# A hybrid attention and MLP block: the column-tile jobs of w1 in one place, the last k norm ahead of the LN2 statistics, one V drain back on ScalarE

## The chip, the core and the metric

The kernel runs on one core of one Trainium2 chip. The metric is the device time of one launch in microseconds (us). The core's engines work from queues of their own and meet at semaphores: TensorE (PE) multiplies matrices and writes PSUM, VectorE (DVE) and ScalarE (ACT) drain PSUM and do elementwise work, GpSimd (POOL) does elementwise work in SBUF, and SyncE (SP) issues most DMAs.

## The reference

The input x has 2048 tokens of width 448. It is normalised, and two branches are added to it:

```python
xn = layernorm(x)
# A: linear attention, 16 heads of 28
q, k, v = split(xn @ wqkv)
phi_q = concat(softmax(q @ w_phi), softmax(-(q @ w_phi)))   # phi_k alike
kv = phi_k.T @ v ;  z = sum(phi_k) ;  o = (phi_q @ kv) / (phi_q @ z + 1e-6)
A = o @ wo
# B: token mixing and an MLP, on xn
h  = gelu(layernorm(xn) @ w1)                # 448 -> 448
hs = concat(h[:, 0:112] shifted by 1 token, h[:, 112:224] by -1,
            h[:, 224:336] by 2, h[:, 336:448] by -2) @ w2
x1 = xn + hs
B  = x1 + gelu(layernorm(x1) @ w3) @ w4      # 448 -> 1792 -> 448
out = x + A + B
```

## The kernel before

The 2048 tokens are 16 tiles of 128, in groups g of four tiles. Activations are also kept transposed (`xnT`, `hT`, `gT`), so that they can be a matmul's operand. Nearly all matmuls use half of TensorE's rows: a job works on a pair of PSUM banks, with the two row halves running beside each other (64x128 tiles). Each such job comes in two halves, written V(i,0) and V(i,1) below; the second half exchanges rows and banks, and so waits until the matmuls of the first half have ended. There are four pairs of PSUM banks, numbered 0 to 3. A job can start on a pair only when the engine that drains the pair's last job has read it.

The program is a list of operations in the order in which Python calls them; each engine gets its own operations in that order, and a recorder sets the semaphore waits from what each operation reads and writes. So the order of the calls is the order of every queue. Nothing is reordered by a scheduler.

The stages, in order of time:

1. *Front, about 5 to 32 us.* `ln1_stats` and `ln1_apply` normalise x. `xn_T` transposes tiles on TensorE into a bank pair, and ScalarE copies them out (DVE for tiles 10 and 11, in pair 1). Then jobs follow from a list written by hand: V (`v_pair`, x times wv, drained by `v_out` into `vaug`), WA (`wa_pair`, columns 0 to 255 of w1 for one group, drained by `wa_out` with gelu), WC (`wc_pair`, columns 256 to 383, drained by `wc_out`), WD (`wd_pair`, the last 64 columns for half of the tokens, drained by `wd_out`), and FO (`fold_pair`, which folds w_phi into the k and q weights; DVE copies the results to `wpk` and, in four copies a job, to `wpq`). WD is the only job that uses column tiles as well: four 64x64 tiles side by side. Its first half has 16 matmuls, its second 12.
2. *Shifts.* `hop_out`, `hop_in` and `halo` move small strips of `hT` by DMA on SP, in two halves h; the loads of w3, wo and w4 stand behind them in SP's queue.
3. *Eight k/q rounds, about 32 to 69 us.* Round `ps` multiplies k of tiles 2ps and 2ps+1 (pair 1), q (pair 0), and one w2 job (pair 2; V of tiles 12 and 13 in round 0, and V of tiles 14 and 15 in pair 3 beside it). ScalarE takes exp of both signs of k (`k_exp`) and of q (`q_exp`). `k_norm` then sums k's exponentials on DVE (`ksum`), takes the reciprocal on DVE (`rks`) and multiplies on POOL. `w2_out` adds the w2 job to xn on DVE for two tiles (i and i+4), and `ln_stats` takes the LN2 statistics of one tile a round, also on DVE. `ln_scale` turns statistics into scales on POOL (`mv`, `rs`), `g_apply` normalises a tile into `g_tok`, and `g_T` transposes it into `gT` by DMA on SP. `kv_tile` adds phi_k and v of one tile into pair 3.
4. *MLP and output, from about 69 us.* w3 jobs (`a(p)`, `b(p)`) with gelu on ScalarE, the last kv tiles (`K(...)`), `kv_copy` (DVE reads the kv banks), `kv_blocks`, then the numerators (`N`) and the four-part output jobs (`f`).

In the trace each helper has one line: L200 a matmul, L204 a transpose on TensorE, L208 a ScalarE activation, L212 an elementwise operation on DVE or POOL, L215 a DMA transpose, L218 a DMA. So operations are told apart by tile names and shapes. In these names, `w` stands for w1 and what shares its region (the kv copies) as well as for w2, w3 and w4; `g_tok,hi` are the folds; `phik` written by ScalarE from 72 us on is the w3 gelu, which shares phi_k's memory.

At the end of the rounds the calls are:

```python
if ps == 7:
    for i in (6, 7):
        ln_stats(st2, mv2, xn, i)
    ln_scale(mv2, rs2, 4, 4, 0)
k_norm(2 * ps)
```

and the MLP stage begins with `g_apply` of tiles 4 to 7 on DVE, ahead of `kv_copy` in DVE's queue.

Of the kernel before, what the change touches and what calls it, by code (L numbers as in the profile page):

```python
# [220 lines left out]
def bass_parallel_sum__linear_kernel_hedgehog__mixer_s_mlp__prompt_kernel(  # L221
# [14 lines left out]
    with es:  # L236
# [14 lines left out]
        def new(name, cols, dt=BF16):  # L251
            return view(region(name, cols * DTB[dt]), cols, dt)
# [10 lines left out]
        xn = new("xn", NT * 512).rearrange("p (t d) -> p t d", t=NT)  # L263
# [37 lines left out]
        st2 = new("st2", NT * 8, F32).rearrange("p (t c) -> p t c", t=NT)  # L301
        mv2 = new("mv2", NT * 8, F32).rearrange("p (t c) -> p t c", t=NT)
        rs2 = new("rs2", NT * 8, F32).rearrange("p (t c) -> p t c", t=NT)
# [36 lines left out]
        dve, pool = "DVE", "POOL"  # L340
# [90 lines left out]
        def ln_stats(stt, mvt, src, i):  # L431
            R.ew(dve, "bn_stats", stt[:, i, 0:6], src[:, i, 0:D])
            R.ew(dve, "bn_aggr", mvt[:, i, 0:2], stt[:, i, 0:6])

        def ln_scale(mvt, rst, a, n, neg):
            R.ew(pool, "tensor_scalar", mvt[:, a:a + n, 2], mvt[:, a:a + n, 1], LN_EPS, 1.0, op0=ALU.add, op1=ALU.mult)
            R.ew(pool, "tensor_tensor", rst[:, a:a + n, 0], mvt[:, a:a + n, 2], mhalf[:, 0:n], op=ALU.pow)
            if neg:
                R.ew(pool, "tensor_scalar", rst[:, a:a + neg, 1], mvt[:, a:a + neg, 0], -1.0, 0.0, op0=ALU.mult,
                     op1=ALU.add)  # L440
# [64 lines left out]
        def two(b):  # L505
            return pairs[b // 2].rearrange("p (b e) -> p b e", b=2)
# [3 lines left out]
        def row_pairs(first, second, start=False, cols=1):  # L510
            for s, (p, q) in enumerate(zip(first, second)):
                for out, lhs, rhs in (p, q) if cols == 1 else (*p, *q):
                    R.mm(out, lhs, rhs, start and s == 0, False)

        def lap_pair(outs, lhs, rhs):
            def side(k, rows, kcs):
                return [(outs[k], lhs(k, kc, *rows), rhs(k, kc, *rows)) for kc in kcs]
            return (lambda: row_pairs(side(0, LO, (0, 1, 2, 3)), side(1, HI, (0, 1, 2, 3)), True),
                    lambda: row_pairs(side(1, LO, (0, 1, 3)), side(0, HI, (0, 2, 3))))

        def k_pair(i, b):
            return lap_pair([banks[2 * b + k][:, 0:D] for k in range(2)],
                            lambda k, kc, lo, hi: xnT[lo:hi, kc, 128 * (i + k):128 * (i + k) + 128],
                            lambda k, kc, lo, hi: wpk[lo:hi, kc, :])

        def q_pair(g, c, b):
            return lap_pair([banks[2 * b + k] for k in range(2)],
                            lambda k, kc, lo, hi: wpq[lo:hi, kc, 128 * (c + k):128 * (c + k) + 128],
                            lambda k, kc, lo, hi: xnT[lo:hi, kc, 512 * g:512 * g + 512])
# [6 lines left out]
        def v_out(i, b, eng="ACT"):  # L536
            vd = vaug[:, i:i + 2, :].rearrange("p t (h e) -> p t h e", e=HP)[:, :, :, 0:DH]
            vs = two(2 * b)[:, :, 0:D].rearrange("p t (h e) -> p t h e", e=DH)
            if eng == "ACT":
                R.act(vd, vs, ACT.Copy)  # L540
            else:
                R.ew(dve, "tensor_copy", vd, vs)

        def wa_pair(g, b):
            return lap_pair([banks[2 * b + k] for k in range(2)],
                            lambda k, kc, lo, hi: w1[lo:hi, kc, 128 * k:128 * k + 128],
                            lambda k, kc, lo, hi: xnT[lo:hi, kc, 512 * g:512 * g + 512])
# [4 lines left out]
        def wc_pair(g, b):  # L552
            return lap_pair([banks[2 * b + k][:, 0:256] for k in range(2)],
                            lambda k, kc, lo, hi: w1[lo:hi, kc, 256:384],
                            lambda k, kc, lo, hi: xnT[lo:hi, kc, 512 * g + 256 * k:512 * g + 256 * k + 256])
# [4 lines left out]
        def wd_pair(h, b):  # L560
            def side(k, q, rows, kcs):
                lo, hi = rows
                t0 = 512 * (2 * h + q) + 256 * k
                return [(banks[2 * b + k][64 * q:64 * q + 64, 0:256], w1[lo:hi, kc, 384:448], xnT[lo:hi, kc, t0:t0 + 256])
                        for kc in kcs]
            up, down = (0, 1, 2, 3), ((0, 1, 3), (0, 2, 3))
            return (lambda: row_pairs([*zip(side(0, 0, LO, up), side(0, 1, LO, up))],
                                      [*zip(side(1, 0, HI, up), side(1, 1, HI, up))], True, 2),
                    lambda: row_pairs([*zip(side(1, 0, LO, down[0]), side(1, 1, LO, down[0]))],
                                      [*zip(side(0, 0, HI, down[1]), side(0, 1, HI, down[1]))], False, 2))  # L570
# [58 lines left out]
        def kv_tile(i):  # L629
            def side(k, rows):  # L630
                return [(banks[6 + k][:, 64 * n:64 * n + HP + DH + 2],
                         phik[rows[0]:rows[1], i, 4 * n:4 * n + 4, :].rearrange("p g e -> p (g e)"),
                         vaug[rows[0]:rows[1], i, 64 * n:64 * n + HP + DH + 2]) for n in range(8)]
            row_pairs(side(0, LO), side(1, HI), i == 0)
# [165 lines left out]

        vps = {i: v_pair(i, b) for i, b in ((0, 2), (2, 3), (4, 3), (6, 1), (8, 1), (10, 1), (14, 3))}
        was = {g: wa_pair(g, b) for g, b in ((0, 0), (1, 0), (2, 0), (3, 2))}
        wcs = {g: wc_pair(g, b) for g, b in ((0, 2), (1, 3), (2, 0), (3, 0))}
        wds = {h: wd_pair(h, b) for h, b in ((0, 2), (1, 3))}
        fps = {(t, m): fold_pair(t, m, b) for t, m, b in ((1, 0, 3), (1, 2, 2), (0, 0, 2), (0, 2, 3))}

        def V(i, k):
            return (vps[i][k],)

        def WA(g, k):  # L810
            return (was[g][k],)

        def WC(g, k):
            return (wcs[g][k],)

        def WD(h, k):
            return (wds[h][k],)

        def FO(t, m, k):
            return (fps[t, m][k],)  # L820
# [4 lines left out]
              WA(0, 1), (xn_t, 6, 1, 0), WC(0, 0), (xn_t, 7, 1, 1), (xn_e, 6, 1, 2), WC(0, 1), (wa_out, 0, 0), (wc_out, 0, 2),  # L825
              V(4, 0), V(6, 0), V(4, 1), (v_out, 4, 3), V(6, 1), (v_out, 6, 1),
              WA(1, 0), (xn_T, 8, 2, 2), WC(1, 0), WA(1, 1), (xn_T, 10, 1, 2, "DVE"), (ln1_end,), WC(1, 1), (wc_out, 1, 3),
              (wa_out, 1, 0), WD(0, 0), V(8, 0), WD(0, 1), (wd_out, 0, 2), V(8, 1), (v_out, 8, 1),
              FO(1, 0, 0), WA(2, 0), FO(1, 0, 1), FO(1, 2, 0), WA(2, 1), (wa_out, 2, 0), FO(1, 2, 1),
              V(10, 0), (xn_T, 14, 3, 2), V(10, 1), (v_out, 10, 1), FO(0, 0, 0), WC(2, 0), FO(0, 0, 1), FO(0, 2, 0),  # L830
              WC(2, 1), (wc_out, 2, 0), FO(0, 2, 1), WA(3, 0), WC(3, 0), WA(3, 1), (wa_out, 3, 2), WD(1, 0),
              WC(3, 1), (wc_out, 3, 0), WD(1, 1), (wd_out, 1, 3)])
        for h in range(2):
            hop_out(h)
            hop_in(h)
# [12 lines left out]
        for ps in range(8):  # L848
            k, q = k_pair(2 * ps, 1), q_pair(ps // 2, 2 * (ps % 2), 0)
            w = (w2_pair if ps else v_pair)(side[ps], 2)  # L850
            k[0]()
            if ps > 2:
                kv_tile(2 * ps - 6)
                kv_tile(2 * ps - 5)
            w[0]()
            k[1]()
            for s in range(2):
                k_exp(2 * ps, 1, s)
            q[0]()
            w[1]()  # L860
            if ps:
                w2_out(side[ps], 2)
            else:
                v_out(12, 2, "DVE")
                vps[14][0]()
            q[1]()
            for s in range(2):
                q_exp(2 * ps, 0, s)
            if not ps:
                vps[14][1]()  # L870
                v_out(14, 3, "DVE")
            if ps in (3, 5):
                ln_scale(mv2, rs2, ps - 3, 2, 2)
                for i in (ps - 3, ps - 2):
                    g_apply(i)
                    g_T(i)
            if ps == 7:
                for i in (6, 7):
                    ln_stats(st2, mv2, xn, i)
                ln_scale(mv2, rs2, 4, 4, 0)  # L880
            k_norm(2 * ps)
            if 0 < ps < 7:
                ln_stats(st2, mv2, xn, ps - 1)

        w3p = [w3_pair(p) for p in range(28)]
        fp = [fin_pair(2 * k) for k in range(7)]
# [21 lines left out]
        def G(*t):  # L908
            return (lambda: [g_T(i) for i in t],)
# [4 lines left out]
        def A(*t):  # L914
            return (lambda: [g_apply(i) for i in t],)

        play([
            *[(g_apply, i, dve) for i in (4, 5, 6, 7)], G(4, 5, 6, 7),
            a(0), (wl[11][0],), b(0), a(1), K(10, 11), b(1), K(12), a(2), K(13), b(2), a(3), K(14, 15), b(3), (kv_copy,),
            a(4), (w2_last, 11), b(4), a(5), (kv_blocks,), b(5),  # L920
            a(6), N(0), (w2_norm, 8), b(6), a(7), f(1, 0), b(7), N(1), (w2_norm, 10), A(8, 9, 10, 11),
# [52 lines left out]
```

The softmax here doesn't subtract the row's maximum and nothing guards it: scores larger than these inputs give would overflow.

## Time and profile before

| what | value |
|---|---|
| median of 9 runs | 176.94 us (176.88 to 177.47) |
| time of the profiled execution | 177.17 us |
| its span in the profile | 175.4 us |
| granted TensorE clock | 0.998 |
| PE busy | 169.1 us, 96% of the span |
| DVE, POOL, ACT busy | 116.1, 91.7, 81.3 us |
| chain of waits: share of PE | 87% |

The span is the time from the first to the last profiled instruction; the execution's own time has 1.8 us around it. Starts are given in us from the span's start. A matmul's start is recorded and its end is modelled, so work on PE is best read from start to start. PEld is the loading of weights, which runs ahead of the matmuls; a wait shown on PEld becomes a wait of PE only when the matmuls before it have run out. A chain of waits tells, step by step, what the last-ending work hung on; work that is not on it has something to hide behind.

### The profile page before, as it was taken

What the parts mean: (1) busy time and instruction counts of PE and PEld (TensorE: products, weight loads), DVE (VectorE), ACT (ScalarE), POOL (GpSimd) and SP (SyncE); (2) the same over time, 40 slices, a digit from 0 to 9 for tenths busy, and PEclk for the clock granted to TensorE, in tenths of its full rate; (3) what the DMA queues carried; (4) which work ended last, traced back from release to release, by engine and by line L of the source; (5) the groups of instructions that cost most, each with busy time, mean ns of one, the idle gap of its engine ahead of it and who ended that gap; (6) DMA issues with size and microseconds to landing.
All of it is one profiled execution on the core that took longest, in us unless ns stands there. A gap on an engine that the chain in (4) does not pass through costs nothing.

```text
span 175.4 us, 5174 instructions
## 1 busy us (share of the span) xinstructions
PE 169.1 (96%) x2254; PEld 89.9 (51%) x2254; DVE 116.1 (66%) x259; ACT 81.3 (46%) x93; POOL 91.7 (52%) x129
## 2 busy tenths in 40 slices
PE   7799999999999999989999999999999999999993
PEld 5456576554555554544454554555545555545451
DVE  4799976169999999995776971544427425474621
ACT  2269864877877777937224422223214222224000
POOL 4676570004979999660458389460720714523740
PEclk9999999999999999999999999999999999999999
DMA  5999332118961102025012642034411220312331
GB/s 167 340 212 128 108 69 54 35 33 298 386 211 34 30 17 47 4 50 74 4 30 49 74 92 55 31 86 90 93 30 52 59 56 4 84 34 30 82 102 32
DMA packets 32678, 15.20 MB, mean 87 GB/s; under 512 B 24080, under 2 KB 32016, under 8 KB 32656
## 3 DMA queue, kind: packets, MB, share of 16 engines
q1 hardware_dynamic: 29888, 12.96, 32.4%
q10 hardware_dynamic: 2768, 1.92, 3.5%
q8 instruction: 17, 0.28, 0.7%
q14 instruction: 5, 0.04, 0.1%
HBM read 7.14 MB, written 1.84 MB: 51 GB/s over the span
## 4 chain that ended last, share of the span: by engine, by line
PE 87%; DVE 4%; DMA 3%; POOL 2%; SPq 1%; issue 0%; ACT 0%; DVEq 0%
PE bank L200 86%; DMA xtok<-in_A_x_dram 3%; POOL phik L212 2%; DVE ksum L212 1%; PE bank L204 1%; DVE st L212 1%; DVE xn L212 1%; DVE wpq L212 1%; SPq L218 1%; ACT xnT L208 0%; DVE rks L212 0%; DVE mv L212 0%; DVE vaug L212 0%; DVEq L173 0%
## 5 line engine op out<-in xcount | busy, mean ns | idle before, releaser
L208 ACT ACTIVATE phik<-bank 128x1024 bf16<-128x1024 f32 (+1 forms) x44 | 42.3, 984 | 62.1 <-PE bank L200 62.1
L200 PE MATMUL bank<-gT,w 64*128 64x512 bf16 x392 | 50.0, 377 | 0.0
L212 DVE TENSOR_TENSOR vaug<-bank,vaug 128x464 f32<-128x464 f32 (+3 forms) x65 | 32.6, 512 | 23.0 <-PE bank L200 21.3
L200 PE MATMUL bank<-w,phik 64*128 64x448 bf16 (+1 forms) x420 | 45.0, 349 | 0.0
L212 POOL TENSOR_TENSOR xnT<-vaug 128x196 bf16<-128x196 f32 (+1 forms) x32 | 18.1, 587 | 46.8 <-DVE vaug L212 46.8
L200 PEld LDWEIGHTS bank<-w,phik 64*128 64x128 bf16 (+1 forms) x420 | 21.7, 94 | 21.2 <-issue 0.4
L212 POOL TENSOR_TENSOR phik<-phik,rks 128x1792 bf16<-128x1792 bf16 x8 | 25.6, 3214 | 11.6 <-DVE rks L212 11.6
L200 PEld LDWEIGHTS bank<-gT,w 64*128 64x128 bf16 x392 | 17.6, 94 | 17.5 <-ACT phik L208 0.4
L212 POOL TENSOR_TENSOR vaug<-xn,xtok 128x448 f32<-128x448 bf16 x16 | 16.2, 1034 | 0.2 <-DVE vaug L212 0.2
L212 DVE TENSOR_REDUCE ksum<-phik 128x64 f32<-128x1792 bf16 x8 | 16.1, 2008 | 0.0
L212 DVE RECIPROCAL vaug<-bank 128x16 f32<-128x16 f32 x16 | 4.1, 257 | 17.9 <-PE bank L200 17.9
L200 PE MATMUL bank<-xnT,wpq 64*128 64x512 bf16 x112 | 14.7, 376 | 0.0
L200 PE MATMUL bank<-xnT,w 64*128 64x256 bf16 (+2 forms) x168 | 14.1, 307 | 0.3 <-DVE wpq L212 0.2
L200 PE MATMUL bank<-wv,xnT 64*128 64x448 bf16 x112 | 13.5, 351 | 0.1
L212 POOL TENSOR_TENSOR rs<-mv,mhalf 128x1 f32<-128x1 f32 (+2 forms) x19 | 12.6, 665 | 1.6
L200 PE MATMUL bank<-wo,xnT 64*128 64x448 bf16 (+1 forms) x106 | 13.4, 349 | 0.0
L200 PE MATMUL bank<-w,hT 64*128 64x448 bf16 x112 | 13.2, 349 | 0.0
L200 PE MATMUL bank<-wpk,xnT 64*128 64x448 bf16 x112 | 13.2, 349 | 0.0
L212 DVE TENSOR_TENSOR xn<-bank,xn 128x512 bf16<-128x512 f32 (+1 forms) x16 | 9.1, 613 | 1.8 <-PE bank L200 1.8
L212 DVE BATCH_NORM_STATS2 st<-xtok 128x6 f32<-128x448 bf16 x16 | 9.9, 617 | 0.5 <-DMA xtok<-in_A_x_dram 0.4
L208 ACT ACTIVATE xnT<-bank 128x512 bf16<-128x512 bf16 x12 | 6.7, 595 | 5.8 <-PE bank L204 5.6
L208 ACT ACTIVATE hT<-bank 128x512 bf16<-128x512 f32 (+1 forms) x10 | 7.3, 769 | 4.4 <-PE bank L200 4.4
(64 smaller groups left out, 171.0 us busy)
## 6 DMA issues: line engine op xcount, KB each, us to landing
w<-in_B_w_dram SPq DMA_DIRECT2D x2, 896.0 KB, 5.8
out_dram<-vaug SPq DMA_DIRECT2D x15, 112.0 KB, 1.9
w<-in_B_w_dram SPq DMA_DIRECT2D x1, 1568.0 KB, 11.3
xtok<-in_A_x_dram ACTq DMA_DIRECT2D x2, 448.0 KB, 8.6
xtok<-in_A_x_dram SPq DMA_DIRECT2D x2, 224.0 KB, 6.4
w<-in_B_w_dram ACTq DMA_DIRECT2D x2, 224.0 KB, 6.5
wo<-in_A_wo_dram SPq DMA_DIRECT2D x2, 224.0 KB, 7.0
w<-in_B_w_dram SPq DMA_DIRECT2D x1, 336.0 KB, 3.5
```

What stands on the lines that cost most here:

```text
L200: self.op("PE", lambda e: e.matmul(out, lhsT, rhs, start=start, stop=stop, skip_group_check=True), [out], [lhsT, rhs], tile=self._tile(lhsT))
L204: self.op("PE", lambda e: e.transpose(out, in_, ident), [out], [in_, ident], tile=self._tile(in_))
L208: self.op("ACT", lambda e: e.activation(out, in_, func, **kw), [out], [in_] + aps)
L212: self.op(eng, lambda e: getattr(e, name)(out, *args, **kw), [out], aps)
L218: self.op(eng, lambda e: e.dma_start(out, in_), [out], [in_], dma=True)
```

## The change

Three things are moved. The number of matmuls, drains and DMAs stays; POOL gets two small instructions more, since one `ln_scale` over four tiles becomes two over two tiles each.

- The WD jobs: WD(0) stood around V(8), WD(1) at the end of the list between WA(3) and WC(3). Now all four halves stand together, behind the last fold and ahead of WA(3). WD(0) uses bank pair 1 instead of 2, WD(1) pair 0 instead of 3, and WC(3) pair 3 instead of 0. FO(1,0,0) takes the place between the halves of V(8).
- The last `k_norm` (tiles 14 and 15) is called ahead of the LN2 statistics of tiles 6 and 7. The scales of tiles 4 and 5 are made ahead of it, those of 6 and 7 behind it, and the applies are split accordingly.
- The drain of V(14) in round 0 goes from DVE to ScalarE, between `q_exp(0)` and `k_exp(2)` in ScalarE's queue.

```diff
-        wcs = {g: wc_pair(g, b) for g, b in ((0, 2), (1, 3), (2, 0), (3, 0))}
-        wds = {h: wd_pair(h, b) for h, b in ((0, 2), (1, 3))}
+        wcs = {g: wc_pair(g, b) for g, b in ((0, 2), (1, 3), (2, 0), (3, 3))}
+        wds = {h: wd_pair(h, b) for h, b in ((0, 1), (1, 0))}
...
-              (wa_out, 1, 0), WD(0, 0), V(8, 0), WD(0, 1), (wd_out, 0, 2), V(8, 1), (v_out, 8, 1),
-              FO(1, 0, 0), WA(2, 0), FO(1, 0, 1), FO(1, 2, 0), WA(2, 1), (wa_out, 2, 0), FO(1, 2, 1),
+              (wa_out, 1, 0), V(8, 0), FO(1, 0, 0), V(8, 1), (v_out, 8, 1),
+              WA(2, 0), FO(1, 0, 1), FO(1, 2, 0), WA(2, 1), (wa_out, 2, 0), FO(1, 2, 1),
               V(10, 0), (xn_T, 14, 3, 2), V(10, 1), (v_out, 10, 1), FO(0, 0, 0), WC(2, 0), FO(0, 0, 1), FO(0, 2, 0),
-              WC(2, 1), (wc_out, 2, 0), FO(0, 2, 1), WA(3, 0), WC(3, 0), WA(3, 1), (wa_out, 3, 2), WD(1, 0),
-              WC(3, 1), (wc_out, 3, 0), WD(1, 1), (wd_out, 1, 3)])
+              WC(2, 1), (wc_out, 2, 0), FO(0, 2, 1), WD(0, 0), WD(1, 0), WD(0, 1), (wd_out, 0, 1), WD(1, 1), (wd_out, 1, 0),
+              WA(3, 0), WC(3, 0), WA(3, 1), (wa_out, 3, 2), WC(3, 1), (wc_out, 3, 3)])
...
             if not ps:
                 vps[14][1]()
-                v_out(14, 3, "DVE")
+                v_out(14, 3)
...
             if ps == 7:
-                for i in (6, 7):
-                    ln_stats(st2, mv2, xn, i)
-                ln_scale(mv2, rs2, 4, 4, 0)
+                ln_scale(mv2, rs2, 4, 2, 0)
             k_norm(2 * ps)
-            if 0 < ps < 7:
-                ln_stats(st2, mv2, xn, ps - 1)
+            for i in ((), (0,), (1,), (2,), (3,), (4,), (5,), (6, 7))[ps]:
+                ln_stats(st2, mv2, xn, i)
...
-            *[(g_apply, i, dve) for i in (4, 5, 6, 7)], G(4, 5, 6, 7),
+            (g_apply, 4, dve), (g_apply, 5, dve), G(4, 5), (ln_scale, mv2, rs2, 6, 2, 0), (g_apply, 6, dve), (g_apply, 7, dve), G(6, 7),
```

## The prediction

> **What bounds the kernel now.** I read the page first (busy shares), then the chain of waits in order of time (where the end is not set by TensorE), then the timeline around those places. TensorE (PE) is busy 169.1 of 175.4 us and holds 87% of the chain, so only places where PE stands still, or does something that is not needed, are worth time. The chain in order of time shows two behind the first 20 us:
>
> ```profile
> 27.38 1.30 DVE wpq L212 x4
> 28.68 0.05 issue
> 28.72 40.03 PE bank L200 x557
> ...
> 71.33 2.00 DVE ksum L212
> 73.33 0.02 issue
> 73.35 0.56 DVE rks L212
> 73.91 0.07 issue
> 73.98 3.23 POOL phik L212
> 77.21 0.05 issue
> 77.26 95.40 PE bank L200 x1166
> ```
>
> Read: start, length, what. From 28.72 to 68.76 PE alone carries the chain, so the eight k/q rounds are bound by PE. At 27.38 PE hangs on four VectorE (DVE) copies, at the end of the rounds on the last k norm (sum on DVE, reciprocal, multiply on GpSimd, POOL). From 77.26 to the end it is PE again: what is gained before it is gained at the end. The timeline of the first place:
>
> ```profile
> 20.04 0.76 DVE L212 COPY xnT<-bank 128x512 bf16<-128x512 bf16 x2
> 20.26 0.36 PEld L200 LDWEIGHTS bank<-xnT,w 64*64 64x64 bf16 x16 [0.21 <-issue]
> 20.85 0.49 PEld L200 LDWEIGHTS bank<-wv,xnT 64*128 64x128 bf16 x8 [0.23 <-DVE xnT L212]
> 21.72 0.25 PEld L200 LDWEIGHTS bank<-xnT,w 64*64 64x64 bf16 x12 [0.37 <-issue]
> 22.17 0.30 PEld L200 LDWEIGHTS bank<-wv,xnT 64*128 64x128 bf16 x6 [0.20 <-issue]
> 28.72 1.63 PEld L200 LDWEIGHTS bank<-xnT,w 64*128 64x128 bf16 x21 [0.50 <-DVE wpq L212]
> ```
>
> The rows marked 64*64 are the column-tile jobs: WD(0,0) at 20.26, WD(0,1) at 21.72. V(8,0) at 20.85 waits for the DVE copies of 20.04, not for WD. And of the second place:
>
> ```profile
> 71.33 1.99 DVE L212 TENSOR_REDUCE ksum<-phik 128x64 f32<-128x1792 bf16 x1
> 73.82 4.18 DVE L212 TENSOR_SCALAR g_tok<-xn,mv,rs 128x512 bf16<-128x512 bf16 x4
> 73.98 3.22 POOL L212 TENSOR_TENSOR phik<-phik,rks 128x1792 bf16<-128x1792 bf16 x1 [1.18 <-DVE rks L212]
> 74.86 1.69 PE L200 MATMUL bank<-gT,w 64*128 64x512 bf16 x14
> 77.26 0.51 PEld L200 LDWEIGHTS bank<-vaug,phik 64*128 64x128 bf16 x32 [1.21 <-POOL phik L212]
> ```
>
> PE has no work left at 76.55 and waits for POOL's multiply, which waited for a sum that stood behind the LN2 statistics of tiles 6 and 7.
>
> **What the skill says.** (1) "TensorEngine Tiling (Array Packing)", Tiling Modes, Key Properties: changing the tiling mode drains TensorE. The trace agrees: V(8,0), eight matmuls, would end its issue at 20.86+0.77=21.63 (the same shape takes 32.22 to 32.98), WD(0,1) starts at 21.72: 0.09 going in; its three rounds of four matmuls at 0.11 would end at 22.07, V(8,1) starts at 22.17: 0.10 going out. With the slower first round a job costs about 0.22 in switches. (2) "SBUF — State Buffer", Who interferes with whom: DVE in a two-port mode and POOL share a port pair as an exclusive lock, the loser blocks. It agrees: one of the four g_tok applies above takes 3.30 us beside POOL's 3.22 multiply, the others 0.32 to 0.40. (3) "ScalarE: Activation LUTs", What ACT_TABLE_LOAD costs, about 1283 ns; here 1.28 at 32.98.
>
> **The change, part by part.** (Times before from the timeline, instruction by instruction; "now" is worked out.)
>
> *a. WD(0,0) and WD(0,1) leave the place around V(8).* WD(0,0) filled the wait for the DVE copies (end 20.80): taking it out gains nothing, V(8,0) stays at 20.86. After it come FO(1,0,0), 0.11, at 21.63 and V(8,1), which must wait for V(8,0)'s last matmul (start 21.44, 0.35 long) and 0.06 for the semaphore (as V(0,1) did at 8.59): 21.85 instead of 22.17. V(8,1) takes 0.58, so WA(2,0) is at 22.43 instead of 22.86 (FO's 0.11 is moved, not removed): **-0.43**. Up to the end of FO(0,2,1) every wait in the stretch (wpk copies, transposes, ScalarE drains) is fed by PE itself and moves along. The weight transposes for FO(1,0,0) were issued from 5.5 on and take at most 7.0 to land, so 21.63 is late enough.
>
> *b. Both WD jobs ahead of WA(3).* PE is free at 27.41 instead of 27.84. WD(0,0) needs bank pair 1, drained by ScalarE's V copy (27.96 before, now 27.53): start 27.58. WD(1,0) needs pair 0 from the WC(2) gelu (28.50 before, now 28.07): start 28.12, a stall of about 0.1. Then 0.45, 0.33, 0.33 and the exit drain: WA(3,0) at 29.32. Before, it was held by the wpq copies to the equal of 28.62. So here **+0.70**: 0.78 of waiting is replaced by 1.91 of work and short waits, less the 0.43.
>
> *c. The tail loses WD(1,0) and WD(1,1).* These held 30.67 to 31.33 and 31.67 to 32.22 with their drains, 1.21; the rows' stagger of half a matmul costs 0.1 of that. WA(3,0) 0.87, WC(3,0) 0.44, WA(3,1) 0.64, WC(3,1) 0.33 from 29.32: K(0) at 31.60 instead of 32.22, **-0.62** in all of a to c. WC(3) now uses pair 3, drained by the last wpq copy at 29.42, before 30.19.
>
> *d. ScalarE at the entry of the rounds.* The WA(3) gelu now comes last but one: 31.47 to 32.49. V(12,0) on its pair 2 could start at 32.37 and starts at 32.54: **+0.17**. Gelu of WC(3) to 33.0, table load 1.28, first k exp at 34.30 (34.51 before), done 36.03, needed at 37.26: hidden. On SP's queue the second half of the hops waits for these gelus about 0.6 longer (33.0 instead of 32.5); the halo and the weight loads stand behind it. First users of that half are the w2 pair at about 52 (halo) and 56, of w3 at 69: hidden by over 10 us.
>
> *e. V(14)'s drain from DVE (1.09) to ScalarE (0.92, the bf16 copy's row).* It queues behind the q exps (36.94 to 38.88) and ahead of the second k exps: 38.78 to 39.70. They could start at 39.55 and start at 39.60; K(4), which waits for them, has about 0.1 to spare. Cost 0 to 0.1, taken 0.05. Its reader is the kv product of tile 14, near 76. DVE starts its first k sum 1.1 earlier and its w2 sums are ready sooner: the small waits of 42.69 and 44.07 (0.06, 0.04) go at most: taken -0.05. The rounds then run 0.45 earlier throughout.
>
> *f. The last k norm first.* At w2's last add DVE ends at 69.93-0.45=69.48; sum 1.99, reciprocal 0.55: 72.0. POOL is busy without a break up to 71.37-0.45=70.92, then the split scale of tiles 4 and 5 (0.20 and 0.71 as at 52.78) to 71.9. The multiply runs 72.05 to 75.27 instead of 73.98 to 77.20. Unheld, the kv matmuls start 0.21 after their weight load and that 0.12 after the last load (76.04), as at 73.24 and 73.45: 76.37 in the old clock instead of 77.26: **-0.89**. In the new clock the load is due at 75.7, 0.4 after the multiply.
>
> *g. What is queued behind.* DVE: statistics to 73.5, the applies of 4 and 5 blocked by POOL's lock to 75.3, done 76.0; POOL's second scale 75.3 to 76.4 (two instructions more than before); applies of 6 and 7 to 77.1; kv_copy, behind them, 77.1 to 78.5 (77.92 to 79.37 before). Its reader on PE stood at 81.31, now due 79.97: 1.5 to spare, cost 0. SP: the four transposes that follow the applies take 1.2 to 1.8 each to issue and 2.5 to land; from 77.1 the last lands by about 83 and is read near 87: cost 0. The gelu that frees the bank of the next w3 pair (76.74 before, moves 0.45) is due at 76.47 now: a stall of up to 0.05, not counted.
>
> **Sum.** -0.62+0.17+0.05-0.05-0.89 = **-1.34**. Against the profiled execution's own 177.17 (span 175.41, 1.76 around it) that is 175.83. The median of the nine runs, 176.94, is 0.23 lower: 175.6. Bounds: a to e between -0.1 (block waits fully for both drains, ring pays for the V copy) and -0.75; f between -0.7 (only PE's own idle, 0.72) and -1.0. A measurement here can tell about 0.2% (0.35 us) from no change.
>
> **The rivals.**
> 1. *Only the end gains (chance 0.17).* The front trades one fill for another: WD(0,0) no longer fills the copy wait, 1.5 us of WD work lands where only 0.8 was idle, ScalarE's drains hold the block. For it: the 0.1 and 0.17 stalls above sit on ScalarE. Against it: six of eight mode switches go. -0.9: 176.05.
> 2. *Only the front gains (0.07).* POOL's multiply is not earlier, or PE stops just behind on the gelu or kv_copy. Against it: POOL is free at 70.9 and DVE's sum has no other input than exps done at 68.6. -0.45: 176.5.
> 3. *Slower: DVE's queue ahead of kv_copy (0.07).* The applies of 6 and 7 now wait for a POOL scale that stands behind the multiply, and two-port DVE work and POOL lock each other out. PE's kv_blocks wait swallows all gains ahead of it: it costs from a kv_copy end of 79.9 on, and the kernel is slower than before from about 81.6, which is one further hold of a multiply's length (3.2) over my 78.5: 177.3. For it: the 3.30 us apply; against it: after 75.3 POOL has only 0.9 us of short work queued.
> That the change does something else than it says is excluded: each engine's instruction stream differs as described, SP's not at all.
>
> **How the numbers follow.** The forecast above has 0.69, with 175.2 to 175.9 its own range. Range: 175.1 to 176.5, which takes in rivals 1 and 2. Faster by over 0.2%: nearly all of forecast and rivals 1 and 2, 0.89; within: 0.04; slower: 0.07.
>
> **What would show it.** No 64*64 rows before 27; V(8,0) still near 20.86; one run of 64*64 rows of about 1.7 us from 27.5, and no wait on wpq; K(0) near 31.6; a V copy on ScalarE near 38.8; POOL's last multiply from about 72; no PE wait on POOL near 75.7; kv_copy near 77. Wrong would be: a wait on wpq or on ScalarE of over 0.4 around 27 to 33, rounds longer than 4.61 us (K(8) to K(10) now), or a PE wait at kv_blocks.

## Result, and the profile after

The changed kernel takes 175.92 us (median of 10 runs, 175.68 to 176.62) against 176.99 (median of 32). The ratio is 0.9937, with a 95% interval of 0.9928 to 0.9947: 0.94 to 1.27 us faster. Forecast were 175.6, and a gain of 1.34. Run again later, beside other kernels, it took 175.97 against 176.95 (0.9949, 0.9931 to 0.9967). The profiled execution took 175.79 us, its span is 174.0.

The chain that ended last (section 4 of the page of the changed kernel) is now 94% TensorE, before 87%. Before it held 2% of POOL and 4% of DVE. Not all of the seven points are the change's: the chain reaches TensorE at 9.45 us before and at 6.75 after, ahead of all that was moved. Its shares now:

```profile
PE 94%; DVE 3%; issue 1%; POOL 0%; ACT 0%; DVEq 0%
```

In order of time (start, us, what) one piece of it waits on DVE around V(8); the four wpq copies, and the last norm's sum, reciprocal and multiply, are gone from it:

```profile
19.89 0.77 DVE xnT L212 x2
20.65 0.05 issue
20.70 4.39 PE bank L200 x60
...
27.38 5.06 PE bank L200 x92
32.44 0.04 issue
32.48 138.79 PE bank L200 x1790
```

The break at 32.48 is V(12,0), which waits for the WA(3) gelu. The timeline of the front:

```profile
20.70 0.93 PE L200 MATMUL bank<-wv,xnT 64*128 64x448 bf16 x8 [0.53 <-DVE xnT L212]
27.38 0.36 PEld L200 LDWEIGHTS bank<-xnT,w 64*64 64x64 bf16 x16
27.92 1.11 PEld L200 LDWEIGHTS bank<-xnT,w 64*64 64x64 bf16 x40 [0.17 <-ACT hT L208]
29.23 2.17 PEld L200 LDWEIGHTS bank<-xnT,w 64*128 64x128 bf16 x28 [0.20 <-DVE wpq L212]
32.47 0.49 PEld L200 LDWEIGHTS bank<-wv,xnT 64*128 64x128 bf16 x8 [0.47 <-ACT hT L208]
```

There is one run of 64*64 rows from 27.38 on, and V(8) still stands at 20.70, now behind 0.53 us of idle PE. The view puts the 0.20 ahead of WA(3,0), at 29.23, down to the wpq copies. They can't be the cause: the eight copies follow one another from 26.75 to 29.22, and the first four, which drain WA(3)'s pair, were through at 28.03. The last 64x64 matmul starts at 29.03, so the 0.20 is its 0.11 and the way back to 64x128 tiles. The wait on wpq is gone, as forecast. The end of the rounds:

```profile
69.35 2.01 DVE L212 TENSOR_REDUCE ksum<-phik 128x64 f32<-128x1792 bf16 x1
72.03 3.21 POOL L212 TENSOR_TENSOR phik<-phik,rks 128x1792 bf16<-128x1792 bf16 x1
73.30 2.42 DVE L212 TENSOR_SCALAR g_tok<-xn,mv,rs 128x512 bf16<-128x512 bf16 x2
75.67 0.71 PEld L200 LDWEIGHTS bank<-vaug,phik 64*128 64x128 bf16 x32
76.34 0.74 DVE L212 TENSOR_SCALAR g_tok<-xn,mv,rs 128x512 bf16<-128x512 bf16 x2 [0.63 <-POOL rs L212]
77.00 0.67 DVE L212 COPY w<-bank 128x496 f32<-128x496 f32 x1
```

The sum stands right behind w2's last add, the multiply starts at 72.03 instead of 73.98, and the weight load of the last kv tiles waits for nobody.

Executions differ in their first microseconds by some tenths, whichever the kernel. To compare stages, the table gives places counted from the first DVE copy of tile 10 (20.04 before, 19.89 after); nothing ahead of it is changed in any of these kernels. Each row is one profiled execution. K(0) and K(4) are the first matmuls of k in rounds 0 and 2 (tiles 0 and 1, 4 and 5), "last kv tiles" is the code's `K(14, 15)`, and the first w3 job on tiles 4 to 7 is `a(7)`.

| kernel | V(8,0) | K(0) | K(4) | last kv tiles | kv_blocks | first w3 job on tiles 4 to 7 | last matmul |
|---|---|---|---|---|---|---|---|
| before | 0.81 | 12.17 | 21.83 | 57.22 | 61.27 | 63.90 | 152.25 |
| changed | 0.81 | 11.63 | 21.49 | 55.99 | 60.04 | 62.67 | 151.02 |
| end only | 0.81 | 12.17 | 21.82 | 56.34 | 60.38 | 63.29 | 151.66 |
| front only | 0.81 | 11.64 | 21.49 | 56.88 | 60.94 | 63.57 | 151.93 |
| V drain only | 0.81 | 12.17 | 21.83 | 57.21 | 61.27 | 63.91 | 152.26 |
| V(8) on pair 2 | 0.12 | 11.23 | 21.09 | 55.59 | 59.64 | 62.79 | 151.15 |
| f(1,0) first | 0.81 | 11.63 | 21.49 | 55.99 | 60.04 | 65.32 | 151.03 |
| both of these | 0.12 | 11.23 | 21.08 | 55.59 | 59.64 | 64.92 | 150.65 |
| both, round 0 | 0.12 | 11.23 | 21.11 | 55.62 | 59.67 | 64.95 | 150.68 |
| split block | 0.81 | 11.86 | 21.72 | 56.23 | 60.27 | 62.90 | 151.26 |
| kv_copy late | 0.81 | 11.63 | 21.48 | 55.99 | 60.54 | 63.19 | 151.54 |
| WD(1) moved alone | 0.81 | 11.50 | 21.35 | 55.86 | 59.90 | 63.03 | 151.39 |

So the change is worth 1.23 us in these places: 0.34 by K(4), the other 0.89 by the last kv tiles, and nothing is given back to the last matmul. The changed kernel run again has the same places within 0.01.

### The profile page after: what moved, and what is told of

Read it like the earlier page. It is cut to its first block, busy times and chain, and to the rows that moved or that the text cites. A ratio compares the mean times of both kernels' runs of the same rounds, so it can differ in the third digit from the quotient of the medians.

```text
span 174.0 us, 5178 instructions
## 1 busy us (share of the span) xinstructions
PE 168.8 (97%) x2254; PEld 90.4 (52%) x2254; DVE 114.2 (66%) x258; ACT 81.9 (47%) x94; POOL 92.4 (53%) x131
## 4 chain that ended last, share of the span: by engine, by line
PE 94%; DVE 3%; issue 1%; POOL 0%; ACT 0%; DVEq 0%
PE bank L200 92%; PE bank L204 1%; DVE vaug L212 1%; DVE st L212 1%; DVE xnT L212 0%; DVE xn L212 0%; ACT xnT L208 0%; POOL rs L212 0%; DVE mv L212 0%; DVEq L173 0%; DVE gT L212 0%; POOL mv L212 0%
## 5 line engine op out<-in xcount | busy, mean ns | idle before, releaser
L200 PE MATMUL bank<-xnT,w 64*128 64x512 bf16 (+2 forms) x168 | 13.3, 306 | 0.0
L212 POOL TENSOR_SCALAR g_tok<-xn,rs 128x512 bf16<-128x512 bf16 x12 | 9.1, 772 | 0.3
```

The source lines that it names most:

```text
L200: self.op("PE", lambda e: e.matmul(out, lhsT, rhs, start=start, stop=stop, skip_group_check=True), [out], [lhsT, rhs], tile=self._tile(lhsT))
L212: self.op(eng, lambda e: getattr(e, name)(out, *args, **kw), [out], aps)
```

## Experiments

**The parts alone.** Each kernel is the kernel before with one part of the diff.

```diff
 # end only: k_norm(14) ahead of the statistics, split scale and applies
 # front only: the list of jobs and the bank pairs of WC(3) and WD
 # V drain only:
-                v_out(14, 3, "DVE")
+                v_out(14, 3)
```

> Only the k norm of tiles 14 and 15 ahead of the LN2 statistics, with the split scale and applies; front and V drain as before. Theory (sum of parts): the end is worth 0.89 us (the PE wait of 1.21 on weights ahead of the last kv matmuls goes), so about 176.1 us, 0.995 of before. Rival (only the end gains, the front is a trade): the whole gain of 1.1 us is here, 175.9 us. Rival (a later wait swallows it): nearer 176.6 us, with a new wait on PE between 76 and 81 us.

> Only the column-tile jobs moved, with their bank pairs; end and V drain as before. Theory: V(8,0) where it was, K(0) 0.5 to 0.6 earlier, V(12,0) held about 0.3 by the WA(3) gelu, rounds 0.35 to 0.45 earlier, wait on POOL at the end unchanged: about 176.55 us. Rival (a trade of one fill for another): within 0.1 us of before.

> Only the V(14) drain goes from DVE to ScalarE. Theory: 0 plus or minus 0.1 us, since the rounds are bound by PE and ScalarE has 0.7 us to spare ahead of the second k exps, less than the drain's 0.9, so that K(4) may start up to 0.2 later. Rival (ScalarE's ring has no spare): 0.2 to 0.9 us slower.

Measured: the end alone 176.44 us (ratio 0.9957, 0.9941 to 0.9973), the front alone 176.65 (0.9963, 0.9949 to 0.9977), the V drain alone 176.93 (0.9995, 0.9985 to 1.0005), against 177.09. By the table the end is worth 0.88 by the last kv tiles, the front 0.34, the drain nothing, and 0.88+0.34 is the 1.23 of both but for 0.01. The rivals "only the end" and "a trade" fall: the front's interval lies wholly under 1. But the end alone gave back 0.3 later, between kv_blocks and the first w3 job on tiles 4 to 7 (2.91 us apart instead of 2.63). So it took 176.44 where 176.1 was expected. That wait was neither forecast nor in the range of 76 to 81 us that the expectation names.

**V(8) on another bank pair.** This one asks whether the idle 0.53 us ahead of V(8) is the price of taking WD(0,0) away, and can be bought back.

```diff
-        vps = {... (8, 1), (10, 1), (14, 3))}
+        vps = {... (8, 2), (10, 1), (14, 3))}
-              ... V(8, 1), (v_out, 8, 1),
+              ... V(8, 1), (v_out, 8, 2),
```

> The changed kernel with V(8) on bank pair 2 instead of 1. Pair 2 is free since the column-tile jobs left it, so V(8,0) need not wait for the DVE copies of tiles 10 and 11. Theory (the wait of 0.53 us on PE at 20.7 is the price of taking WD(0,0) away, and it is a bank's): V(8,0) 0.5 earlier, WA(2,0) held 0.1 to 0.2 by the WA(1) gelu, in all 0.3 to 0.5 us faster than the changed kernel, about 175.5 us. Rival (the front is held by something else, normalising or ScalarE's drains): no difference from the changed kernel, the time lost again before K(0).

V(8) started 0.69 earlier (0.12 instead of 0.81), and 0.40 of it was left at K(0), K(4), the last kv tiles and kv_blocks: the wait was one for a bank. Yet the time, 175.86 us (0.9929, 0.9908 to 0.9949), isn't clearly under the changed kernel's, and in the profile all 0.40, and 0.13 more, were lost at one place. The timeline of that run:

```profile
81.62 0.33 PEld L200 LDWEIGHTS bank<-gT,w 64*128 64x128 bf16 x6
82.77 0.57 PEld L200 LDWEIGHTS bank<-gT,w 64*128 64x128 bf16 x8 [0.82 <-issue]
82.80 1.04 PE L200 MATMUL bank<-gT,w 64*128 64x512 bf16 x8 [0.35 <-DMA gT<-g_tok]
```

The eight matmuls at 82.80 are the first w3 job on tiles 4 to 7. PE stands idle 0.35 us until the last of the four DMA transposes has landed; counted from start to start, the job comes 0.51 later than the pace of the matmuls before it. SP's queue in the timeline of the changed kernel, the issue of the four:

```profile
75.42 5.59 SPq L215 DMA_TRANSPOSE gT<-g_tok  x4
```

And in that of V(8) on pair 2:

```profile
75.14 6.19 SPq L215 DMA_TRANSPOSE gT<-g_tok  x4
```

Counted from the DVE copies, the four begin 0.40 earlier and are all issued 0.20 later. The last landed at 82.23 in the changed kernel, 0.33 ahead of its reader; before, at 82.93, 1.02 ahead. Where the job was held, it started 0.13 to 0.25 after the landing (V(8) on pair 2, end only, WD(1) moved alone), so no more than 0.1 to 0.2 of the 0.33 was to spare. The slack there was nearly used up by the change, and any further gain ahead of it runs into these transposes.

Why they take so long is told in part by the DMA queues between 75 and 78.5 us. The answer for the changed kernel (packets, MB, share of 16 engines):

```profile
q8 instruction: 1, 0.02, 1.7%
```

And for V(8) on pair 2:

```profile
q8 instruction: 1, 0.02, 2.5%
```

One fetch of 16 KB of instructions falls into each stretch. A share of 1.7% of 16 engines over 3.5 us is 0.95 us, 2.5% is 1.40. The first of the four transposes landed 3.54 and 4.02 us after its issue, against 2.4 to 2.5 where nothing else runs (the last of the four, and the first before).

The traces of all thirteen profiled executions fit this. In ten of them the fetch begins about 1 us after the issue of the first transpose: where it took 0.93 to 1.11 us (five of them), that transpose landed after 3.54 to 3.60, where it took 1.20 to 1.45 (the other five), after 3.87 to 4.10. In the other three (before, front only, V drain only) the fetch begins later, at 78.0 to 78.7, and there the first transpose took 2.45 and the second, then in flight, 3.6 to 4.3. Still, no run moved the fetch alone: that it delays the transposes is argued, not shown.

If it does, the wait on gT differs from execution to execution of one kernel. The three profiled executions in which PE waited there (end only, V(8) on pair 2, WD(1) moved alone) all had a long fetch, the two of the changed kernel a short one. The 0.3 that the end alone gave back and the 0.53 lost here are then the price in these executions, and not fixed costs of these kernels.

**The w3 job later.** If the wait on gT is what hides gains, work put ahead of the job must bring them out.

```diff
-            ... b(6), a(7), f(1, 0), b(7), N(1), (w2_norm, 10), A(8, 9, 10, 11),
+            ... b(6), f(1, 0), a(7), N(1), (w2_norm, 10), b(7), A(8, 9, 10, 11),
```

> The changed kernel once more, beside the next three on one chip. Theory (gT late): its first w3 job on tiles 4 to 7 has only about 0.3 us in hand after the last of the four gT transposes, so some executions wait there and the median gain is 0.1 to 0.2 us under the 1.23 that the aligned profiles show: about 1.1 us under before, with a last transpose landing between 82.0 and 82.8. Rival (no such wait): 1.2 to 1.3 under before.

> The changed kernel with the first output part f(1,0), 2.8 us of matmuls, ahead of the first w3 job on tiles 4 to 7 (and the numerators N(1) between that job's halves). Theory (gT late): the job then has 3 us in hand, no wait on gT, 0.05 to 0.3 us faster than the changed kernel. Rival (gT hidden anyway): no difference, or slower by a new wait of f(1,0) for the sixth w3 gelu or of N(1) for its queries.

> V(8) on bank pair 2 as before in that experiment, and f(1,0) ahead of the first w3 job on tiles 4 to 7. Theory: the 0.39 us that V(8) on pair 2 had won by the last kv tiles (aligned at the DVE copies) and lost again at gT is now kept: 0.35 to 0.65 us under the changed kernel, no wait on gT. Rival (the front gain is lost elsewhere): as the run with V(8) on pair 2 alone.

> As the last one, and in round 0 the q job's first half takes the place of V(12)'s, so that V(12), whose bank pair is drained by the WA(3) gelu, comes 0.8 us later. Theory: the 0.2 us that PE waits there at 32.4 go, another 0.1 to 0.2 us faster. Rival: the wait turns up at the exps, because ScalarE's table load still ends near 34.2: no difference.

The last one's edit, on top of the other two:

```diff
-            w[0]()
+            (w if ps else q)[0]()
             k[1]()
...
-            q[0]()
+            (q if ps else w)[0]()
             w[1]()
```

Measured against 176.95, in one series: the changed kernel 175.97 (0.9949, 0.9931 to 0.9967), f(1,0) first 175.75 (0.9936, 0.9919 to 0.9953), both 175.50 (0.9914, 0.9899 to 0.9930), both with round 0 175.33 (0.9907, 0.9894 to 0.9920). With V(8) on pair 2 *and* f(1,0) first, the last matmul is at 150.65 instead of 151.02: 0.37 of the 0.40 won at V(8) is kept, and the interval lies under that of the changed kernel. In this execution the transposes had landed early, 0.19 ahead of the job's old place, so the run with round 0 changed too is the stricter one: its last transpose landed 0.20 after the old place (62.50, against 59.67+2.63 from the DVE copies), and the last matmul is at 150.68 all the same.

For the changed kernel alone the reordering changes nothing in the profile (151.03), as PE didn't wait for gT in either of its profiled executions. In the first of them the weights of that job came without a break. In the second they came late, though not late enough to hold PE (the view says "issue", as it does where gT held the job):

```profile
82.45 0.65 PEld L200 LDWEIGHTS bank<-gT,w 64*128 64x128 bf16 x8 [0.21 <-issue]
```

That fits a job at the edge. Whether other executions wait there, as the theory had it, the overlapping intervals leave open.

In round 0 the rival was right about the result and wrong about the cause. V(12,0) no longer waits for the WA(3) gelu, but V(12,1) now follows it without a job between, and waits for its own first half:

```profile
34.33 1.06 PEld L200 LDWEIGHTS bank<-wv,xnT 64*128 64x128 bf16 x14 [0.50 <-PE bank L200]
```

PE loses 0.23 there (34.34 instead of 34.11), about what it had won. K(4) comes at 21.11 instead of 21.08. The 175.33 beside 175.50 is within what the runs differ by.

**The price of a mode switch.**

```diff
-              ... WD(0, 0), WD(1, 0), WD(0, 1), (wd_out, 0, 1), WD(1, 1), (wd_out, 1, 0),
-              WA(3, 0), WC(3, 0),
+              ... WD(0, 0), WD(1, 0), WA(3, 0), WD(0, 1), (wd_out, 0, 1), WD(1, 1), (wd_out, 1, 0),
+              WC(3, 0),
```

> The changed kernel with WA(3,0) put between the column-tile halves WD(1,0) and WD(0,1): the same work, two mode switches more. Theory (a switch drains PE, 0.1 to 0.12 each): K(0), aligned at the DVE copies of tiles 10 and 11, about 0.2 us later than the 11.63 of the changed kernel, 11.83. Rival (switches cost nothing here, the drain was the wait for a bank): no difference, or earlier because WA(3,0) fills the wait of WD(1,0) for its bank.

K(0) is at 11.86: 0.23 later for one switch out and one in, where 0.2 was expected. The trace has 0.09 more than the pace at each switch, and some hundredths in the first matmuls behind it. It agrees with the 0.22 a job that the prediction read off, and fits what the Trainium skill says of a drain ("TensorEngine Tiling (Array Packing)", Tiling Modes).

**Is it WD(0) or WD(1)?**

```diff
-        wds = {h: wd_pair(h, b) for h, b in ((0, 1), (1, 0))}
+        wds = {h: wd_pair(h, b) for h, b in ((0, 2), (1, 1))}
-              ... V(8, 0), FO(1, 0, 0), V(8, 1), (v_out, 8, 1), WA(2, 0), ...
+              ... WD(0, 0), V(8, 0), WD(0, 1), (wd_out, 0, 2), V(8, 1), (v_out, 8, 1), FO(1, 0, 0), WA(2, 0), ...
-              ... WD(0, 0), WD(1, 0), WD(0, 1), (wd_out, 0, 1), WD(1, 1), (wd_out, 1, 0), ...
+              ... WD(1, 0), WD(1, 1), (wd_out, 1, 1), ...
```

> The changed kernel with WD(0) back around V(8) (pair 2) and only WD(1) ahead of WA(3) (pair 1). Theory (WD(0,0) lies free in the wait for the DVE copies; what counts is that the wait for wpq is filled and the tail freed): WA(2,0) 0.43 later than in the changed kernel, WD(1) held to 28.0 by the V(10) drain and its second half to 28.7 by its first, WA(3,0) near 29.1, K(0) at 11.5 to 11.7 from the DVE copies, so the same as the changed kernel's 11.63 within 0.1. Rival (six saved switches are what counts): K(0) 0.4 later, at 12.0.

K(0) is at 11.50, 0.13 *earlier* than in the changed kernel. The loads of this run show why (PEld rows):

```profile
20.04 0.36 PEld L200 LDWEIGHTS bank<-xnT,w 64*64 64x64 bf16 x16 [0.21 <-issue]
20.64 0.49 PEld L200 LDWEIGHTS bank<-wv,xnT 64*128 64x128 bf16 x8 [0.23 <-DVE xnT L212]
...
27.79 0.46 PEld L200 LDWEIGHTS bank<-xnT,w 64*64 64x64 bf16 x16
28.58 0.26 PEld L200 LDWEIGHTS bank<-xnT,w 64*64 64x64 bf16 x12 [0.33 <-PE bank L200]
29.04 2.17 PEld L200 LDWEIGHTS bank<-xnT,w 64*128 64x128 bf16 x28 [0.20 <-DVE wpq L212]
```

WD(0,0) again lies in the wait for the DVE copies, and WD(1) alone fills the wait for wpq, with 0.33 of self-wait between its halves (the 0.20 ahead of 29.04 is again the way back from the 64x64 tiles; the pair's copies were through at 28.45). FO(1,0,0) stands in its old place, and six of the eight switches remain. So the whole front gain is WD(1)'s move from the tail into that wait, and the rival, that saved switches are what counts, falls. Moving WD(0) as well, with the pairs that go with it, costs 0.13. This kernel too lost its further gain at gT (3.13 us from kv_blocks to the job instead of 2.63).

**The margin of kv_copy.** An unused DVE sum is put ahead of it.

```diff
+        def extra():
+            ph = phik[:, 14:16, :, 0:DH].rearrange("p t g e -> p (t g) e")
+            R.ew(dve, "tensor_reduce", ksum[:, 0:2, :].rearrange("p b c -> p (b c)"), ph, axis=AX.X, op=ALU.add)
...
-            ... (g_apply, 7, dve), G(6, 7),
+            ... (g_apply, 7, dve), G(6, 7), (extra,),
```

> The changed kernel with one more DVE sum (2.0 us, its result unused) ahead of kv_copy, so that kv_copy ends near 80.45 instead of 78.45. Theory (margin of about 1.5 us ahead of kv_blocks): the matmuls of kv_blocks are held by 0.5 to 0.6 us and everything behind them by as much. Rival (no margin): 2.0 us later. Rival (more margin than I read): no difference.

From the timeline of that run:

```profile
79.65 0.68 DVE L212 TENSOR_TENSOR w<-bank,w 128x496 bf16<-128x496 f32 x1
80.38 0.38 PE L200 MATMUL bank<-w 64*128 64x232 bf16 x4 [0.34 <-DVE w L212]
```

kv_blocks comes 0.50 later (60.54 instead of 60.04), and the last matmul 0.52: of 2.0 us, 1.5 were hidden. The slower rival had its price right, but needs 1.5 us of lateness before it costs anything.

## Why the prediction was right, and where its terms were off

The forecast was right in sign, place and mechanism, and the time lies in the range. The time alone would not have shown that: 175.92 is 0.02 outside the forecast's own 175.2 to 175.9, it lies nearer to the 176.05 of rival 1 ("only the end gains") than to 175.6, and the range took in rivals 1 and 2. What decides is that the front alone is faster, and that the places moved by what the steps say. Times of the changed kernel are those of its own execution, 0.15 less than on the clock that the prediction counts on. By its steps:

- *Step a* held. V(8,0) at 0.81 on either side; V(8,1) came at 21.69, which is 21.85 less the 0.15 by which this execution began earlier, and WA(2,0) came 0.44 earlier, forecast 0.43.
- *Steps b and c* held within 0.1: K(0) 0.54 earlier, forecast 0.62. WD(0,0) and WD(1,0) waited for the ScalarE drains as said, and the block ran from 27.38 to 29.23, 1.85 us where 1.74 were worked out. The working had all four tiles restart at 28.12 (27.97 here) behind WD(1,0)'s wait. In the trace one matmul starts at 27.92 and the next three at 28.02; from there on the block keeps the pace that was worked out.
- *Step d* held in kind: V(12,0) waits for the gelu. From K(0) to V(12,0) it is 0.96 instead of 0.77, so 0.19 where 0.17 was forecast. Up to K(2) the front gain is thus 0.34, not 0.45.
- *Step e* held: the drain alone moves no place by more than 0.01, and from K(2) to K(4) it is 4.16 on either side. A cost and a gain of 0.05 that cancel would look like that, and so would none of either.
- *Step f* held to 0.01: 0.89 forecast, 0.88 alone and 0.89 in the changed kernel. The multiply, at 72.03, came 1.80 earlier than before from the DVE copies, forecast 1.93; 0.11 of the difference is what the front fell short.
- *Step g* was right on kv_copy (77.00, which is 77.15 on the prediction's clock, forecast 77.1; margin 1.5 shown) and on the port lock: the apply of tile 4 began at 73.30 and took 2.10 us, until just behind the end of POOL's multiply at 75.24, and the next one 0.40. It was **wrong on gT**. "Read near 87" is the reading that failed: before, the first w3 job on tiles 4 to 7 is the last eight of the row of 14 matmuls shown below, so it starts at 83.95, and at 82.56 now. The landing was misread too: the first two of the four took 3.54 and 3.01 us, not 2.5. Cost 0 came out right for the changed kernel's profiles, but by 0.1 to 0.2 us to spare and not by 4, which is luck.

The row of before that "read near 87" passed over, from the timeline of PE:

```profile
83.29 1.68 PE L200 MATMUL bank<-gT,w 64*128 64x512 bf16 x14
```

So 1.23 of the 1.34 stand in the profile. The 0.11 between them belong to two terms of the front: the block of step b, 0.08 too short, and the wait of step d, 0.02 to 0.03 too short. The medians are 1.07 apart. Their interval reaches to 1.27, so the rest may be the spread of runs. A wait on gT in some of them would look the same; in the two profiles of this kernel PE did not wait there.

The better version that the runs point to is V(8) on pair 2 with f(1,0) first: 175.50 us, 0.9914 of before. WD(0) back in the wait for the DVE copies instead, with f(1,0) first, wasn't tried.

## What to carry to other kernels

When PE is the bound, look for its few waits, and for work that lies elsewhere on its path and fits into them; here WD(1), moved from the tail into a wait of 0.8 us, and a norm put ahead of statistics that nobody was waiting for gave the whole gain. Before moving a job out of a place, see what it was covering: WD(0) was covering a wait, and taking it away cost 0.13. And follow every reader behind the gain to the matmul in a merged row of the timeline that needs it, since a margin of 1 us is soon used up where a DMA moves along by less than its reader (here 0.55 against 1.23).

## What had not been expected of the hardware

A switch between 64x128 and 64x64 tiles and back cost 0.23 us on a stream that otherwise never stops. Behind a wait for a bank, one 64x64 matmul started 0.05 us after the bank had been read and the next three 0.10 us after that one (27.92 and 28.02 in the changed kernel, 27.80 and 27.90 where WD(1) moved alone); without a wait the four started within 0.01. Of two DMA transposes issued 1.2 us apart, the first landed after 3.5 to 4.1 us and the second after 3.0 to 3.7 in the ten executions where an instruction fetch begins between their issues, while the two at 63.77 and 65.01 in the changed kernel took 2.4 and 2.5.
